# A cached attention block at decode: whole units per load, all queries and the MLP first, column tiles for V

## The chip, the cores and the metric

The kernel runs on one core of a Trainium2 chip. The metric is the device time of one execution in microseconds (us), and the figure given is the median of several runs. The profile is that of one execution, recorded by the chip's profiler; its times count from the start of the span.

## The reference

Two tokens (batch 2, one query position each) go through attention over a cache of 8192 keys in 32 heads and through a small MLP whose output gates the attention's output. Cut to what matters:

```python
# x [2,1,512]; k_cache, v_cache [2,32,8192,128]; wq [512,4096]; wo [4096,512]
# w1 [512,1376]; w2 [1376,512]; all float32
xn = layernorm(x)
q = (xn @ wq).reshape(2, 1, 32, 128).transpose(0, 2, 1, 3)
p = softmax(einsum("bhqd,bhkd->bhqk", q, k_cache) * 128 ** -0.5)
s = einsum("bhqk,bhkd->bhqd", p, v_cache).transpose(0, 2, 1, 3).reshape(2, 1, 4096) @ wo
g = silu(gelu(layernorm(xn) @ w1 + b1) @ w2 + b2)
out = x + s * g
```

K and V are 268 MB each and are read once; every byte meets one multiplication and one addition. The weights add some 22 MB.

## The kernel before

A **unit** is one (head, batch) pair: 64 units, unit i being head i // 2 and batch i % 2. K and V of a unit are 4 MB each. They come in two chunks of 2 MB (`CK` = 32 keys per partition, so 16 KB in a row for each of 128 partitions) into pools of four buffers each (`kpool`, `vpool`). All loads are issued by SyncE's queue (SP) in the order of the program; a load whose buffer isn't free yet stops all that stand behind it. K's chunks run three chunks ahead of V's (`LEAD`).

For a unit, VectorE (DVE) multiplies each chunk of K by the head's query, broadcast over the keys (L142), and sums over the 128 elements (L143). The greatest score goes from DVE (L147) through a transpose on TensorE (PE, L149) back to DVE (L154), is spread over the partitions by a product (L156) and copied by ScalarE (ACT, L158), which then takes the exponentials and their sum (L161). The denominator is a product with ones (L182) and a reciprocal (L184).

The products with V (`weighted`, L169) have four columns of exponentials as the stationary operand and four keys of V, 512 columns, as the moving one: 16 products for a unit, which float32 turns into 32 passes, all into the same 4 x 512 block of PSUM. Row r of it holds wanted sums only in its r-th block of 128 columns, which `project` picks: a copy on ACT (L193), four products with columns of the identity (L200), a scaling by the denominator (L203), and, after the second batch of a head, the product with the head's rows of `wo` (L206).

The products of a unit trail its scores: in turn i stand the second chunk of unit i-2, the projection of i-2, the maximum of i-1, and the first chunk of i-1.

The weights share `wpool`, three buffers of 1 MB: `wq` by groups of four heads (1 MB, rows of 2 KB), each loaded four units ahead of the queries that need it (`queries`, L125: sixteen passes of 512 columns for a group, since the token is spread over all 128 partitions so that the query comes out broadcast); `wo` by the same groups; and the MLP in seven parts in units 3 to 9 (`mlp_load`, `mlp_hidden`, `mlp_out`), w1 in rows of 1376 bytes (L218), w2 in rows of 2 KB (L224). The last unit's V comes in nine pieces, three of which DVE multiplies and sums itself (L175, L177).

On each engine the instructions stand in the order that a scheduler in the framework chose from this program.

Of the kernel before, what the change touches and what calls it, by code (L numbers as in the profile page):

```python
# [8 lines left out]
F32 = mybir.dt.float32  # L9
# [4 lines left out]
CK = 32          # keys per partition in one chunk of the cache  # L14
# [6 lines left out]
def decode_kernel(ctx: ExitStack, tc: tile.TileContext, x, kc, vc, wq, wo, w1, b1, w2, b2, out):  # L21
    nc = tc.nc
    P = 128
# [3 lines left out]
    ND = D // P                    # chunks of the model dimension  # L27
    KP = S // P                    # keys per partition
    NCK = KP // CK                 # chunks per (batch, head)
    HG = 512 // DH                 # heads per weight group  # L30
    NU = B * H
    SCALE = float(DH) ** -0.5
    JW = 512 // DH                 # keys per partition in one product with V

    consts = ctx.enter_context(tc.tile_pool(name="consts", bufs=1))
# [4 lines left out]
    ps_o = ctx.enter_context(tc.tile_pool(name="ps_o", bufs=2, space=bass.MemoryType.PSUM))  # L40
    ps_w = ctx.enter_context(tc.tile_pool(name="ps_w", bufs=2, space=bass.MemoryType.PSUM))
    ps_s = ctx.enter_context(tc.tile_pool(name="ps_s", bufs=3, space=bass.MemoryType.PSUM))
    ps_a = ctx.enter_context(tc.tile_pool(name="ps_a", bufs=1, space=bass.MemoryType.PSUM))

# [1 line left out]
    def load_wq(g):  # L46
        t = wpool.tile([P, ND, 512], F32, tag="w", name=f"wq{g}")
        nc.sync.dma_start(t, wq[:, g * 512:(g + 1) * 512].rearrange("(c p) n -> p c n", p=P))
        return t

    def load_wo(g):
        t = wpool.tile([P, HG, D], F32, tag="w", name=f"wo{g}")
        nc.sync.dma_start(t, wo[g * HG * DH:(g + 1) * HG * DH, :].rearrange("(h p) n -> p h n", p=P))
        return t

    def cache_chunk(t, i, c):
        h, b = divmod(i, B)
        return t[b, h, c * P * CK:(c + 1) * P * CK, :].rearrange("(p j) d -> p j d", p=P)

    def load_chunk(pool, src, name, i, c):  # L60
        t = pool.tile([P, CK, DH], F32, tag=name, name=f"{name}{i}_{c}")
        nc.sync.dma_start(t, cache_chunk(src, i, c))
        return t

    K, V, WO = {}, {}, {}
    K[0, 0] = load_chunk(kpool, kc, "k", 0, 0)
    x_sb = consts.tile([B, D], F32, name="x_sb")
    nc.sync.dma_start(x_sb, x.rearrange("b s d -> (b s) d"))
    wq_t = {0: load_wq(0)}
    for c in range(1, NCK):  # L70
        K[0, c] = load_chunk(kpool, kc, "k", 0, c)

# [4 lines left out]
    nc.vector.memset(ones, 1.0)  # L77
    srow = consts.tile([1, P], F32, name="srow")
# [17 lines left out]
    def transposed(src, n, name):  # L96
        # [B, n*128 or less] -> [128, n, B]
        p = ps_w.tile([P, 512], F32, tag="w", name=f"pt_{name}")
        t = consts.tile([P, n, B], F32, name=f"{name}T")
        width = src.shape[1]  # L100
        for c in range(n):
            m = min(P, width - c * P)
            nc.tensor.transpose(p[:m, c * B:(c + 1) * B], src[:, c * P:c * P + m], ident[:B, :B])
        full = width // P
        nc.scalar.copy(t[:, :full, :], p[:, :full * B].rearrange("p (c b) -> p c b", b=B))
        if full < n:
            m = width - full * P
            nc.scalar.copy(t[:m, full, :], p[:m, full * B:(full + 1) * B])
        return t

    xn = layernorm(x_sb, "xn")
    xnT = transposed(xn, ND, "xn")
    xnB = consts.tile([P, ND, B, P], F32, name="xnB")
    for c in range(ND):
        for b in range(B):
            nc.vector.tensor_scalar_mul(xnB[:, c, b, :], ones, xnT[:, c, b:b + 1])

# [1 line left out]
    def queries(g):  # L119
        q = small.tile([P, B, HG, DH], F32, tag="q", name=f"q{g}", bufs=2)  # L120
        w = wq_t.pop(g)
        for b in range(B):
            p = ps_w.tile([P, 512], F32, tag="w", name=f"pq{g}_{b}")
            for c in range(ND):
                nc.tensor.matmul(p, xnB[:, c, b, :], w[:, c, :], start=(c == 0), stop=(c == ND - 1))  # L125
            nc.scalar.copy(q[:, b].rearrange("p h d -> p (h d)"), p)  # L126
        return q

    Q = {0: queries(0)}

# [1 line left out]
    SC, PR, RS, MX, PO, OT = {}, {}, {}, {}, {}, {}  # L132
    PD = {}                         # partial outputs summed on VectorE
    acc = ps_a.tile([B, D], F32, name="acc")

    def scores(i, c):
        h, b = divmod(i, B)
        k = K.pop((i, c))
        if c == 0:
            SC[i] = small.tile([P, KP], F32, tag="sc", name=f"sc{i}")  # L140
# [22 lines left out]
    def weighted(i, v, k0, n, first, last, jw=JW):  # L163
        # products of n keys per partition with V as the moving operand: row r of
        # the output holds the keys k with k % jw == r in its r-th block
        if first:
            PO[i] = ps_o.tile([jw, jw * DH], F32, tag="o", name=f"po{i}")
# [19 lines left out]
    def project(i, direct=()):  # L187
# [8 lines left out]
        for v, k0, n in direct:  # L196
            terms += [(v[:, j, :], PR[i][:, k0 + j:k0 + j + 1]) for j in range(n)]
# [202 lines left out]
```

## Time and profile before

| | us |
|---|---|
| runs shown (three) | 1356.81, 1358.66, 1624.9 |
| their median | 1358.66 |
| span of the profiled execution | 1355.7 |
| DVE busy in it | 1179.7 |
| PE busy in it | 1194.9 |
| ACT busy in it | 111.3 |

The time that was taken of the profiled execution itself isn't shown apart from its span; the median of the runs stands 3.0 us above the span, the lowest run 1.1 us. The run of 1624.9 us is far from the other two, and the profile is not of it.

How to read the profile: a group of instructions is named by line, engine, operation and tiles (`po<-v,pr` writes `po` from `v` and `pr`), then count, busy time, the mean duration of one in ns, the engine's idle time just before them, and what ended it. "SPq" is the queue of loads on SyncE. A product's duration is modelled and overlaps with the next; the pace of a run of products is read from the chain of waits, which gives the time of sixteen together. "PEclk" is the clock granted to TensorE as a share of full speed. The rate in GB/s is that of all sixteen transfer engines.

### The profile page before, as it was taken

To read this page: it belongs to the slowest core of one execution; us is meant where nothing else is said; L and a number is where in the kernel's file an instruction comes from. 1 tells how busy PE (TensorE), PEld (TensorE's weight loads), DVE (VectorE), ACT (ScalarE), POOL (GpSimd) and SP (SyncE) were. 2 spreads that over 40 slices of the span, in tenths; PEclk is the share of its full clock that TensorE was granted. 3 is DMA by queue.
4 is the path that set the end of the run, shared out by engine and by line. 5 is a ranking of instruction groups with operands and counts; after the bars stand their busy time and mean duration, and the time that the engine had idled before them with its cause. 6 is when DMAs were issued, how large, how long until landed. Compare 5 with 4: busy or idle time off the path is not lost.

```text
span 1355.7 us, 7973 instructions
## 1 busy us (share of the span) xinstructions
PE 1194.9 (88%) x3191; PEld 315.5 (23%) x3191; DVE 1179.7 (87%) x491; ACT 111.3 (8%) x363; POOL 0.7 (0%) x6
## 2 busy tenths in 40 slices
PE   3598999899988989899989999899898999889897
PEld 1122222222222222122212222122222222212223
DVE  5968857989998898888989889887988879989998
ACT  0001101010000000001000000001000000000000
POOL 0000000000000000000000000000000000000000
PEclk8788899899999999889999989889988989999998
DMA  9998999999999999999999999999999999999994
GB/s 381 423 383 320 391 393 380 425 430 427 424 430 425 427 428 425 427 424 430 428 425 426 424 430 426 424 429 425 428 427 424 425 429 426 425 429 427 428 428 194
DMA packets 49922, 559.83 MB, mean 413 GB/s; under 512 B 4599, under 2 KB 6647, under 8 KB 17373
## 3 DMA queue, kind: packets, MB, share of 16 engines
q1 hardware_dynamic: 49884, 559.32, 97.9%
q8 instruction: 25, 0.41, 0.1%
q14 instruction: 13, 0.10, 0.0%
HBM read 559.30 MB, written 0.00 MB: 413 GB/s over the span
## 4 chain that ended last, share of the span: by engine, by line
PE 45%; DMA 38%; DVE 13%; ACT 3%; issue 1%; SPq 0%
PE po L169 35%; DMA v<-in_A_v_cache_dram 28%; DMA k<-in_A_k_cache_dram 9%; DVE k L142 6%; DVE sc L143 6%; PE pq L125 4%; PE pt L200 2%; PE acc L206 1%; ACT o L193 1%; PE pl L182 1%; PE pgate L264 1%; DMA x_sb<-in_A_x_dram 1%; ACT oT L203 0%; ACT pr L161 0%; PE pm L149 0%
## 5 line engine op out<-in xcount | busy, mean ns | idle before, releaser
L169 PE MATMUL po<-v,pr 128*4 128x512 f32 (+1 forms) x2076 | 955.4, 616 | 41.9 <-DMA v<-in_A_v_cache_dram 41.9
L142 DVE TENSOR_TENSOR k<-k,q 128x4096 f32<-128x4096 f32 x128 | 565.1, 4415 | 39.7 <-DMA k<-in_A_k_cache_dram 35.4
L143 DVE TENSOR_REDUCE sc<-k 128x32 f32<-128x4096 f32 x128 | 564.2, 4409 | 1.7
L169 PEld LDWEIGHTS po<-v,pr 128*4 128x4 f32 (+1 forms) x2076 | 176.0, 90 | 720.6 <-issue 667.8
L193 ACT COPY o<-po 4x512 f32<-4x512 f32 x64 | 36.4, 570 | 922.9 <-PE po L169 922.9
L200 PE MATMUL pt<-ident,o 4*128 4x1 f32 (+1 forms) x506 | 67.6, 250 | 45.8 <-ACT o L193 45.6
L200 PEld LDWEIGHTS pt<-ident,o 4*128 4x128 f32 (+1 forms) x506 | 62.1, 189 | 102.5 <-ACT o L193 102.0
L154 DVE TENSOR_REDUCE nm<-pm 1x1 f32<-1x128 f32 x64 | 17.6, 274 | 59.6 <-PE pm L149 59.5
L125 PE MATMUL pq<-wq,xnB 128*128 128x512 f32 x128 | 59.6, 617 | 1.3 <-ACT q L126 0.7
L184 DVE RECIPROCAL rl<-pl 128x1 f32<-128x1 f32 x64 | 10.3, 162 | 50.0 <-PE pl L182 50.0
L182 PE MATMUL pl<-rs,ones 128*128 128x1 f32 x128 | 28.0, 288 | 23.6 <-ACT pr L161 23.6
L206 PE MATMUL acc<-wo,oT 128*2 128x512 f32 x64 | 39.8, 709 | 4.0 <-ACT oT L203 0.4
L182 PEld LDWEIGHTS pl<-rs,ones 128*128 128x128 f32 x128 | 22.5, 220 | 60.9 <-ACT pr L161 50.8
L149 PE MATMUL pm<-ident,mx 128*1 128x128 f32 x64 | 17.4, 272 | 21.5 <-DVE mx L147 21.4
L125 PEld LDWEIGHTS pq<-wq,xnB 128*128 128x128 f32 x128 | 24.4, 197 | 30.7 <-issue 27.5
L156 PE MATMUL pb<-nm,srow 1*128 1x1 f32 x128 | 23.5, 250 | 6.2 <-DVE nm L154 6.2
L203 ACT ACTIVATE oT<-pt,rl 128x1 f32<-128x1 f32 x64 | 16.7, 261 | 83.5 <-PE pt L200 83.5
L149 PEld LDWEIGHTS pm<-ident,mx 128*1 128x1 f32 x64 | 5.1, 79 | 76.0 <-issue 48.2
L161 ACT ACTIVATE pr<-sc,bias 128x64 f32<-128x64 f32 x64 | 22.2, 348 | 2.2 <-ACT bias L158 0.2
L156 PEld LDWEIGHTS pb<-nm,srow 1*128 1x128 f32 x128 | 19.8, 192 | 7.4 <-DVE nm L154 6.5
L126 ACT COPY q<-pq 128x512 f32<-128x512 f32 x16 | 9.4, 586 | 113.0 <-PE pq L125 113.0
L147 DVE TENSOR_REDUCE mx<-sc 128x1 f32<-128x64 f32 x64 | 14.0, 219 | 1.1
(63 smaller groups left out, 106.2 us busy)
## 6 DMA issues: line engine op xcount, KB each, us to landing
k<-in_A_k_cache_dram SPq DMA_DIRECT2D x128, 2048.0 KB, 29.2
v<-in_A_v_cache_dram SPq DMA_DIRECT2D x126, 2048.0 KB, 30.3
wq<-in_A_wq_dram SPq DMA_DIRECT2D x8, 1024.0 KB, 29.4
wo<-in_A_wo_dram SPq DMA_DIRECT2D x8, 1024.0 KB, 32.4
v<-in_A_v_cache_dram SPq DMA_DIRECT2D x7, 512.0 KB, 14.8
w<-in_B_w_dram SPq DMA_DIRECT2D x4, 688.0 KB, 5.3
w<-in_B_w_dram SPq DMA_DIRECT2D x2, 1024.0 KB, 5.2
w<-in_B_w_dram SPq DMA_DIRECT2D x1, 512.0 KB, 4.0
```

What stands on the lines that cost most here:

```text
L125: nc.tensor.matmul(p, xnB[:, c, b, :], w[:, c, :], start=(c == 0), stop=(c == ND - 1))
L142: nc.vector.tensor_tensor(out=k, in0=k, in1=qb, op=ALU.mult)
L143: nc.vector.tensor_reduce(out=SC[i][:, c * CK:(c + 1) * CK], in_=k, axis=AX.X, op=ALU.add)
L149: nc.tensor.transpose(p[:1, :], mx, ident)
L154: nc.vector.tensor_reduce(out=nm, in_=MX.pop(i)[:1, :], axis=AX.X, op=ALU.max, negate=True)
L156: nc.tensor.matmul(p[:, :1], srow, nm, start=True, stop=True)
L161: nc.scalar.activation(PR[i], SC.pop(i), AF.Exp, bias=bias, scale=SCALE, accum_out=RS[i])
L169: nc.tensor.matmul(PO[i], PR[i][:, k0 + j:k0 + j + jw], v[:, j:j + jw, :].rearrange("p j d -> p (j d)"), start=(first and j == 0), stop=(l ...
L182: nc.tensor.matmul(pl[:, :1], ones, RS.pop(i), start=True, stop=True)
L193: nc.scalar.copy(o4, po)
L200: nc.tensor.matmul(pt[:, :1], lhsT, rhs, start=(t == 0), stop=(t == len(terms) - 1))
L206: nc.tensor.matmul(acc, OT.pop(h), WO[h // HG][:, h % HG, :], start=(h == 0), stop=(h == H - 1))
```

## The change

**Loads.** A unit's K and its V are one load each: 4 MB, 32 KB in a row for a partition. `kpool` has three such buffers, `vpool` two, `wpool` two of 1 MB for `wo`. In turn i stand the loads of K(i+3) and V(i+1), so K is two units ahead of V.

**Queries and MLP.** `wq` is loaded at the start, in two halves of 4 MB into V's buffers, with four of its rows to a partition; all queries are computed there (`project_q`) in column tiles, four groups of heads side by side on PSUM's partitions 0, 32, 64 and 96, and kept (`q_nat`). For each group `queries` broadcasts them by products with a column of the identity (four passes). w1 is loaded into one of K's buffers and w2 into one of V's. The hidden layer has w1 as the stationary operand: each product takes every tenth column of it, 40 bytes apart, against two columns of the token, so that the hidden values come out on the partitions and need no transposes. The output layer runs in four column tiles of 128 columns.

**Products with V.** The 16 products of a unit go in turn to four column tiles: product t writes the four PSUM partitions from 32 * (t % 4), and there are four such rows of partial sums instead of one. `mask`, four columns with ones at the right rows, sums the tiles in the projection. The product with `wo` and the final gate are in column tiles too, so output and gate lie as [4 x 32, 128].

**The end.** V of the last unit comes in five pieces; 15 products and four keys taken directly (L305); nothing of it on DVE. The last head's rows of `wo` are loaded after V's last piece. The output leaves in four stores from two queues.

**Order.** With `manual_schedule` every engine's instructions stand as the program has them: scores' multiplication of i, the maximum and exponentials of i-1, the sum of i, and then products and projection of i-2.

```diff
-CK = 32          # keys per partition in one chunk of the cache
...
-    kpool = ctx.enter_context(tc.tile_pool(name="kpool", bufs=4))
-    vpool = ctx.enter_context(tc.tile_pool(name="vpool", bufs=4))
-    wpool = ctx.enter_context(tc.tile_pool(name="wpool", bufs=3))
+    kpool = ctx.enter_context(tc.tile_pool(name="kpool", bufs=3))
+    vpool = ctx.enter_context(tc.tile_pool(name="vpool", bufs=2))
+    wpool = ctx.enter_context(tc.tile_pool(name="wpool", bufs=2))
...
+    ctx.enter_context(tc.manual_schedule())
...
+    def load_k(i):
+        K[i] = kpool.tile([P, KP, DH], F32, tag="k", name=f"k{i}")
+        nc.sync.dma_start(K[i], unit(kc, i))
...
+    PIECES = [(0, 16), (16, 16), (32, 16), (48, 12), (60, 4)]
...
+    wq_v = wq.rearrange("(p c) n -> p c n", p=P)
+    for a in range(0, ND, 2):
+        t = vpool.tile([P, 2, H * DH], F32, tag="v", name=f"wq{a}")
+        nc.sync.dma_start(t, wq_v[:, a:a + 2, :])
+        WQ.append(t)
+    load_k(0)
+    w1_sb = kpool.tile([P, ND, F], F32, tag="k", name="w1_sb")
+    nc.sync.dma_start(w1_sb, w1.rearrange("(p c) f -> p c f", p=P))
+    load_k(1)
+    w2_sb = vpool.tile([P, NF + 1, D], F32, tag="v", name="w2_sb")
...
+    load_k(2)
+    load_wo(0)
+    load_v(0)
...
+    def project_q(n):
+        p = ps_w.tile([P, 512], F32, tag="w", name=f"pq{n}")
+        for c in range(ND):
+            for j in range(QT):
+                g = n * QT + j
+                nc.tensor.matmul(p[32 * j:32 * j + B, :], xnT[:, c, :],
+                                 WQ[c // 2][:, c % 2, g * 512:(g + 1) * 512],
+                                 start=(c == 0), stop=(c == ND - 1))
...
+    def mlp_hidden():
+        p = ps_s.tile([P, P], F32, tag="s", name="ph")
+        nc.vector.memset(p[:, :(NF + 1) * B], 0.0)
+        for f in range(NF + 1):
+            for c in range(ND):
+                w = w1_sb[:, c, f:NF * P:NF] if f < NF else w1_sb[:, c, NF * P:]
+                nc.tensor.matmul(p[:w.shape[1], f * B:(f + 1) * B], w, yT[:, c, :],
+                                 start=(c == 0), stop=(c == ND - 1))
...
+    def mlp_out():
+        p = ps_s.tile([P, P], F32, tag="s", name="pgate")
+        nc.tensor.matmul(p, zeros, zeros, start=True, stop=False)
+        for f in range(NF + 1):
+            m = P if f < NF else FT
+            for j in range(QT):
+                nc.tensor.matmul(p[32 * j:32 * j + B, :], hT[:m, f, :], w2_sb[:m, f, j * P:(j + 1) * P],
+                                 start=False, stop=False)
...
+    def weighted(i, t0, t1, nt=NT):
+        po, v = PO[i % 2], V[i]
+        for t in range(t0, t1):
+            j = t % QT
+            nc.tensor.matmul(po[32 * j:32 * j + JW, :], PR[i][:, t * JW:(t + 1) * JW],
+                             v[:, t * JW:(t + 1) * JW, :].rearrange("p j d -> p (j d)"),
+                             start=(t < QT), stop=(t + QT >= nt))
...
+    for i in range(NU + 1):
+        if i + 3 < NU:
+            load_k(i + 3)
+        if i + 1 < NU:
+            if (i + 1) % UG == 0:
+                tail = load_wo((i + 1) // UG)
+            load_v(i + 1)
...
+        if i < NU:
+            scores_mul(i)
+        if i >= 1:
+            max_pe(i - 1)
+            max_dve(i - 1)
+            exps(i - 1)
+        if i < NU:
+            scores_sum(i)
+        if i >= 1:
+            denominator(i - 1)
+        if i == 0:
+            mlp_hidden()
+        if i == 1:
+            mlp_gelu()
+            mlp_out()
...
+        if i >= 2:
+            weighted(i - 2, 0, NT)
+            project(i - 2)
+    i = NU - 1
+    weighted(i, 0, NT - 1, NT - 1)
+    project(i, direct=(KP - JW, KP))
```

More of the change, by code (lines that the diff above doesn't have):

```diff
@@ L81, in decode_kernel @@
     nc.vector.memset(eps_t, EPS)
+    mask = consts.tile([P, JW], F32, name="mask")
+    PO = [ps_c.tile([P, JW * DH], F32, name=f"po{n}") for n in range(2)]
+    for t in PO:
+        nc.vector.memset(t, 0.0)
+    acc = ps_c.tile([P, P], F32, name="acc")
     def layernorm(src, name):
@@ L94, in layernorm, with transposed @@
         return dst
[L96 to L108, printed above, removed]
+    def transposed(src, name):
+        p = ps_s.tile([P, P], F32, tag="s", name=f"pt_{name}")
+        t = consts.tile([P, ND, B], F32, name=f"{name}T")
+        for c in range(ND):
+            nc.tensor.transpose(p[:, c * B:(c + 1) * B], src[:, c::ND], ident[:B, :B])
+        nc.scalar.copy(t, p[:, :ND * B].rearrange("p (c b) -> p c b", b=B))
@@ L129, in decode_kernel @@
[L129 to L136, printed above, removed]
+    nc.vector.tensor_reduce(out=mask, in_=ident.rearrange("p (j r) -> p r j", r=32)[:, :JW, :],
+                            axis=AX.X, op=ALU.add)
+    y = layernorm(xn, "y")
+    xnT = transposed(xn, "xn")
+    yT = transposed(y, "y")
+    q_nat = consts.tile([P, NG // QT, 512], F32, name="q_nat")
+    nc.gpsimd.memset(q_nat, 0.0)
+    def project_q(n):
[6 more added lines that the diff above has]
+                                 start=(c == 0), stop=(c == ND - 1))
+        for j in range(QT):
+            nc.scalar.copy(q_nat[32 * j:32 * j + B, n, :], p[32 * j:32 * j + B, :])
@@ new lines, in decode_kernel, with queries @@
+    Q = {}
+    def queries(g):
+        n, j = divmod(g, QT)
+        q = small.tile([P, B, HG, DH], F32, tag="q", name=f"q{g}", bufs=2)
+        for b in range(B):
+            p = ps_w.tile([P, 512], F32, tag="w", name=f"pb{g}_{b}")
+            r = 32 * j + b
+            nc.tensor.matmul(p, ident[:, r:r + 1].to_broadcast([P, P]), q_nat[:, n, :], start=True, stop=True)
+            nc.scalar.copy(q[:, b].rearrange("p h d -> p (h d)"), p)
+        Q[g] = q
+    project_q(0)
+    queries(0)
+    project_q(1)
@@ L157, in max_b, with exps @@
+    def exps(i):
+        p = ps_s.tile([P, P], F32, tag="s", name=f"pn{i}")
+        nc.tensor.matmul(p[:, :1], srow, MX.pop(i), start=True, stop=True)
         bias = small.tile([P, 1], F32, tag="bias", name=f"bias{i}")
@@ new lines, in project @@
+            for j in range(QT):
+                nc.tensor.matmul(acc[32 * j:32 * j + B, :], oT, w[:, h % HG, j * P:(j + 1) * P],
+                                 start=False, stop=(h == H - 1))
+    for i in range(NU + 1):
[5 more added lines that the diff above has]
+            load_v(i + 1)
+        if i == NU - 2:
+            nc.sync.dma_start(tail[0][:, HG - 1, :], tail[1][:, HG - 1, :])
+        if i < NU:
[13 more added lines that the diff above has]
+            mlp_out()
+        if i == 2:
+            mlp_silu()
+        if i % UG == UG - 2 and i // UG + 1 < NG:
+            queries(i // UG + 1)
@@ L369, in decode_kernel @@
-    r = small.tile([B, D], F32, tag="res", name="res", bufs=1)
+    i = NU - 1
+    weighted(i, 0, NT - 1, NT - 1)
+    project(i, direct=(KP - JW, KP))
+    r = small.tile([P, P], F32, tag="res", name="res", bufs=1)
     nc.vector.tensor_mul(r, acc, gate)
-    nc.vector.tensor_add(r, r, x_sb)
-    nc.sync.dma_start(out.rearrange("b s d -> (b s) d"), r)
+    nc.vector.tensor_add(r, r, x4)
+    for j in range(QT):
+        eng = nc.sync if j % 2 == 0 else nc.scalar
+        eng.dma_start(out[:, 0, j * P:(j + 1) * P], r[32 * j:32 * j + B, :])
```

313 lines of the change are left out of this document (94 added, 219 removed).

## The prediction

> **What bounds the kernel now.** The page came first: the span, the slices of transfer rate and the queue's bytes.
>
> ```profile
> span 1355.7 us, 7973 instructions
> ...
> GB/s 381 423 383 320 391 393 380 425 430 427 424 430 425 427 428 425 427 424 430 428 425 426 424 430 426 424 429 425 428 427 424 425 429 426 425 429 427 428 428 194
> ...
> q1 hardware_dynamic: 49884, 559.32, 97.9%
> ```
>
> The rate is flat from the eighth slice on, lower in the first seven and in the last. A table by stretches (columns: stretch, busy time of PE, weight loads, DVE, ACT, POOL, then granted clock, DMA share, GB/s) prices this:
>
> ```profile
> 3.00:240.00 237.00, 188.52 (x494) 51.43 (x495) 181.93 (x94) 25.54 (x73) 0.00 (x0) 0.88 0.94 386
> 240.00:1320.00 1080.00, 977.51 (x2556) 250.60 (x2554) 968.78 (x378) 81.13 (x277) 0.00 (x0) 0.94 1.01 427
> 1320.00:1338.00 18.00, 17.10 (x65) 5.72 (x64) 16.36 (x8) 2.57 (x9) 0.00 (x0) 1.00 0.95 391
> 1338.00:1356.00 18.00, 11.76 (x82) 7.71 (x79) 12.35 (x10) 0.78 (x3) 0.00 (x0) 0.77 0.05 17
> ```
>
> For 1080 us the transfer engines are never idle: the kernel is bound by its 559.32 MB, which at 427 GB/s take 1309.9 us. The other 46 us are start, stalls and tail. Between 3 and 240 us 386 GB/s instead of 427 lose 237 x 41/427 = 22.8 us; behind the last bytes, at about 1338, stand 17.7 us; the rest is the start and 1.5 us ahead of 1338. Where the 22.8 us go, the transfer slices of the first 240 us (6 us each) and the load queue's own waits say:
>
> ```profile
> GB/s 235 421 406 429 431 350 431 431 406 443 431 426 342 248 429 429 418 352 437 429 300 33 423 429 429 221 407 434 434 307 401 426 436 377 207 394 431 414 431 434
> ```
>
> ```profile
> SPq L62 <- DVE sc L143: 340.7, 57, 23.0
> ...
> SPq L218 <- PE ph L243: 58.7, 3, 22.1
> SPq L224 <- PE pgate L264: 30.1, 2, 18.6
> SPq L224 <- PE ph L243: 19.3, 1, 19.3
> ```
>
> The dips are MLP weight loads (L218, L224) standing at the head of the in-order SP queue until TensorE frees a weight buffer: 108 us of waiting, of which the queue's depth hides all but some 20. The first slice, 235, puts the start of the stream at 6 x (1 - 235/427) = 2.7 us.
>
> **The change, part by part.** Everything is priced by when the next transfer can start.
>
> *Stream.* The bytes stay; rows go from 16 to 32 KB, wq, w1 and w2 from rows of 1.4 or 2 KB to 16 KB and more; only wo keeps 2 KB. No row shows 32 KB. The lower bound is the steady slices in which 2 KB rows still lie, 424; the upper one the 6 us slices at 434. 424 gives 1319.1 us, 434 gives 1288.8. I take 429, nearest to the undisturbed steady slices (427 to 430): 1303.8 us.
>
> *DVE and PE in a unit.* The page's groups, one line of the V tile's own rows, and the chain of waits:
>
> ```profile
> L142 DVE TENSOR_TENSOR k<-k,q 128x4096 f32<-128x4096 f32 x128 | 565.1, 4415 | 39.7 <-DMA k<-in_A_k_cache_dram 35.4
> L143 DVE TENSOR_REDUCE sc<-k 128x32 f32<-128x4096 f32 x128 | 564.2, 4409 | 1.7
> ...
> L193 ACT COPY o<-po 4x512 f32<-4x512 f32 x64 | 36.4, 570 | 922.9 <-PE po L169 922.9
> ...
> L154 DVE TENSOR_REDUCE nm<-pm 1x1 f32<-1x128 f32 x64 | 17.6, 274 | 59.6 <-PE pm L149 59.5
> ...
> L184 DVE RECIPROCAL rl<-pl 128x1 f32<-128x1 f32 x64 | 10.3, 162 | 50.0 <-PE pl L182 50.0
> ...
> L156 PE MATMUL pb<-nm,srow 1*128 1x1 f32 x128 | 23.5, 250 | 6.2 <-DVE nm L154 6.2
> ...
> L161 ACT ACTIVATE pr<-sc,bias 128x64 f32<-128x64 f32 x64 | 22.2, 348 | 2.2 <-ACT bias L158 0.2
> ...
> L147 DVE TENSOR_REDUCE mx<-sc 128x1 f32<-128x64 f32 x64 | 14.0, 219 | 1.1
> ```
>
> ```profile
> L175 DVE TENSOR_TENSOR v<-v,pr x4: 1207/1210/3360, 1330.5 to 1345.9; 128x1024 f32<-128x1024 f32 x3, 128x3072 f32<-128x3072 f32 x1
> ```
>
> ```profile
> 11.76 6.10 PE pq L125 x8
> 17.88 0.59 ACT q L126
> ...
> 86.47 1.06 PE pt L200 x8
> ...
> 384.91 7.04 PE po L169 x16
> ...
> 606.82 6.87 PE pq L125 x16
> ```
>
> From 3072 to 4096 elements a multiply grows by 1.055 us, so 8192 take about 8.7, the reduction the same: 17.4 + 0.27 + 0.16 + 0.22 = 18.1 us of DVE per unit against two loads of 4.19 MB / 429 = 19.6. DVE stays behind the loads with 1.5 us to spare, and may start late: 64 x 18.1 = 1158 us, so unit 63 waits for its K as before. An unpaired product pass costs 7.04/16 = 0.44 us; a unit has 32. One at a time they are 14.1 us, and with about 3 us of small work (the projection's 1.06, the weights' rows and the three single products) they still fit under 19.6. The queries of a group shrink from sixteen passes (6.87 us) to four, a gain on an engine that isn't the bound. How far four column tiles overlap no row shows: bounds 14.1 us and a quarter of it, 3.5. I take about 5, nearer to the low end since the four write different partitions and share no weights.
>
> The Trainium skill, page "TensorE: Matmul & The Clock Gate", section "Measured speedup vs the span model", has three column tiles at 2.38 times one; by that the products would take 14.1/2.38 = 5.9 us, and the sum would be 1 us longer. Against the change speaks its page "TensorEngine Tiling (Array Packing)", section "Key Properties": a change of tiling mode drains TensorE, here twice a unit; no row shows one.
>
> A steady unit on PE, before (L182 the denominator, L169 products of a half unit, L149 the transpose of the maxima, L200 the projection):
>
> ```order
> L182 MATMUL pl_2681<-rs_2679,ones 128x1
> L169 MATMUL po_2687<-v_0_2650,pr_2678 4x512 x8
> L149 MATMUL pm_2698<-ident,mx_2696 1x128
> L169 MATMUL po_2687<-v_1_2702,pr_2678 4x512 x8
> L200 MATMUL pt_2721<-ident,o_41_2719 128x1 x4
> ```
>
> And after (L260 transpose, L270 maximum, L277 denominator, L292 products, L305 projection):
>
> ```order
> L260 MATMUL pm_470<-ident,mx_433 1x128
> L270 MATMUL pn_474<-nm_472,srow 128x1
> L277 MATMUL pl_481<-rs_479,ones 128x1
> L292 MATMUL po_128<-v_277,pr_426 4x512 x16
> L305 MATMUL pt_507<-mask,o_2_505 128x1 x4
> ```
>
> The transpose for unit i-1 now stands behind all products of unit i-3. These begin about 10.5 us after k(i-1) lands (8.7 multiply, 0.3 maximum, 1.5 for the exponentials: two passes of L156, a copy, L161, hand-offs) and end 14.1 + 3 later at worst, 27.6, while DVE reaches its maximum at 19.6 + 8.7 = 28.3. So that wait costs nothing even without overlap; were it late, the K buffers would cover it, since K(i+3) needs the sum of K(i) only some 30 us after it. V(i+1) needs the buffer of V(i-1), freed at the latest 44 us after K(i) landed (28.3 + 1.5 + 14.1) and needed 59 after it (three units on): hidden too. Steady state has no gap.
>
> *Head.* SP's first loads before (wq, wo a group's weights; k, v half units):
>
> ```order
> L62 DMA k_0_82<-in_A_k_cache_dram 128x4096
> L68 DMA x_sb<-in_A_x_dram 2x512
> L48 DMA wq_86<-in_A_wq_dram 128x4x512
> L62 DMA k_1_88<-in_A_k_cache_dram 128x4096
> L53 DMA wo_150<-in_A_wo_dram 128x4x512
> L62 DMA k_0_152<-in_A_k_cache_dram 128x4096
> L62 DMA k_1_154<-in_A_k_cache_dram 128x4096
> L62 DMA v_0_156<-in_A_v_cache_dram 128x4096
> ```
>
> And after, from the second half of wq to the second load of V (k, v whole units; the two w_sb of L90 and L93 are w1 and w2):
>
> ```order
> L86 DMA wq_85<-in_A_wq_dram 128x8192
> L58 DMA k_87<-in_A_k_cache_dram 128x8192
> L90 DMA w_sb<-in_B_w_dram 128x5504
> L58 DMA k_91<-in_A_k_cache_dram 128x8192
> L93 DMA w_sb<-in_B_w_dram 128x5120
> L94 DMA w_sb<-in_B_w_dram 96x512
> L58 DMA k_96<-in_A_k_cache_dram 128x8192
> L64 DMA wo_98<-in_A_wo_dram 128x4x512
> L74 DMA v_100<-in_A_v_cache_dram 128x8192
> L58 DMA k_220<-in_A_k_cache_dram 128x8192
> L74 DMA v_222<-in_A_v_cache_dram 128x8192
> ```
>
> All of wq and the MLP's weights moved into the first dozen loads, sharing K's and V's buffers. Laid end to end from 2.7 us the stream ends: wq 22.2, k0 32.0, w1 38.5, k1 48.3, w2 54.8, k2 64.6, wo 67, v0 76.8, k3 86.6. What frees buffers, with rows for PE's pace:
>
> ```profile
> 1346.22 1.05 PE L200 MATMUL pt<-pr,v 128*128 128x1 f32 x8
> ```
>
> The query projection starts when wq's second half lands at 24: sixteen cold passes at 0.76 are 12.2 us singly, 3 in four tiles; then five copies of 0.59 and four passes, so q is there at 33 to 42. k0 is usable at 34; DVE ends unit 0 at 51.6, in time for k2 (54.8 less some 2 us of issue and landing). Then PE runs the hidden layer, 88 passes at 0.13 us (1.05/8) = 11.5 us with contiguous weights; w1's columns are now 40 bytes apart, which no row shows, so 11.5 to 35 (0.4 each). A gain is excluded, since the loads read no fewer weights. I take 0.2: ends at 69.5, in time for k3 (74.8). But unit 0's transpose stands behind it, so DVE waits: maximum 70, sum 78.7, GELU 81, then 96 output passes of 128 columns at 0.12 (a quarter of 0.44, and the 0.13 of small passes): 92.5. Only then is w2's buffer free for v1: first bytes at 94.5 against 86.6, a gap of 8 us, 2 at 0.13 per pass. Queued behind v1 on SP is everything else, K's loads too. With 1 us of lesser gaps, 9. The 22.8 us of before go. The seven small loads moved to ACT's queue (x, b1, b2) are needed at 79 us or later; the slowest first load of before, x_sb, took 7.29 us, so they are covered tenfold.
>
> *Tail.* Rows of before's end, of its first small load and of a load into an empty queue:
>
> ```profile
> 1349.73 0.27 ACT oT L203
> ...
> 1350.05 1.88 PE acc L206 x2
> ...
> 1351.95 0.69 DVE res L370
> ```
>
> ```profile
> 1.19 7.29 DMA x_sb<-in_A_x_dram
> ```
>
> ```profile
> w<-in_B_w_dram SPq DMA_DIRECT2D x2, 1024.0 KB, 5.2
> ```
>
> ```profile
> 1353.37 0.27 SPq L372 DMA_DIRECT2D out_dram<-res  x1
> ```
>
> The second last gives issue and landing: 5.2 less 1.05 MB / 427 = 2.7 us; the last the store, 1355.7 - 1353.4 = 2.3.
>
> From k63's landing T three V loads are left. v63 waits for the products of unit 61: maximum at T+9, exponentials T+10.5, products T+15.5, with issue and landing T+18 against the end of v62 at T+19.6: a gap of 1 at most. Products 62 end at T+26; those of 63 follow their pieces. Behind the last bytes: landing 2, three products 0.5, copy 0.6, 16 small passes 2, scale 0.3, wo 1, two DVE operations of 128 columns 0.5, store 2.3: 9.2, with the gap 10, instead of 17.7 + 1.5. Were PE still cold, these passes and the products of 61 to 63 take up to twice as long: 20. The DVE sums over V's last pieces, which carried the old tail, are gone; late next is PE's projection.
>
> Sum: 2.7 + 1303.8 + 9 + 10 = 1325.5 us of span. The runs' median, 1358.66, stands 3.0 above the profiled span (the lowest, 1356.81, 1.1 above): **1328 us**.
>
> **Rivals.** *Rows make no difference.* Loads of twice the size stay where steady slices with 2 KB rows lie, 424 to 427, and gains come from head and tail alone: 1309.9 to 1319.1, + 21.7 + 3 = 1335 to 1344. For it: 2 KB rows lower a slice by 3 to 6 GB/s at most, so row length may be no lever. 0.12. The Trainium skill, "DMA: Bandwidth & Descriptors", section "Measured", has 425 GB/s for its largest transfer, 16 MB; by that the time would be 1316.0 + 24.7 = 1341. The trace has 427 with 2 MB, above it already.
>
> *Column tiles don't overlap*, so the change doesn't do what it says. Steady state holds, but the ends lengthen: head 17 (projection of the queries and the output passes serial); in the tail products 61 end at T+24.6, those of 62 at T+43, those of 63 at T+57, and 7 us later, T+64, all ends, where the bytes alone would end at T+30: 34. 2.7 + 1303.8 + 17 + 34 + 3 = 1360, no change. 0.14.
>
> *Strided weights.* At 0.4 us a pass the hidden layer ends at 87, k3 starts 12 us late, v1 14 more: head 26, 1345. 0.13.
>
> *TensorE becomes the bound, slower.* In the stretch
>
> ```profile
> 20.00:40.00 20.00, 1.61 (x7) 0.53 (x6) 20.00 (x5) 0.65 (x2) 0.00 (x0) 0.59 0.99 405
> ```
>
> the clock is 0.59 where PE idles, and eight cold passes took 6.10 us, 0.76 each. If PE idles between units and column-tiled passes run one at a time at that pace, a unit is 32 x 0.76 + 3 = 27.3 us, some 1780 us in all. It decides slower from (20.7 - 3)/32 = 0.55 a pass. Against: work that fills PE was granted 0.94. With mixtures of the two rivals above, 0.09.
>
> **Numbers.** The forecast, 0.52, spans 1308 (434 GB/s, head 4) to 1332. A measurement here tells about 2% from no change: faster means under 1331.5, slower over 1385.8. Faster 0.52, same 0.39 (three rivals), slower 0.09. The range 1308 to 1358 leaves out the slower case, half of the no-overlap case and 0.03 below.
>
> **What would show it.** No slice under 420 GB/s between 110 and 1280 us; steady slices at 429 or more (427 or less: first rival); sixteen products in about 5 us, and within 14 in any case; one gap near 87 us at v1's load, released by the output passes of the MLP; about 9 us behind the last bytes. Wrong would be a steady slice below 420, PE busy all along, or a load queue waiting for PE in steady state.

## The result: 1319.88 us, 0.972 of the time before

| | before | after |
|---|---|---|
| median of the runs, us | 1358.68 | 1319.88 (1317.93 to 1320.07) |
| after / before | | 0.9719, 95% interval 0.9705 to 0.9734 |
| profiled execution: its time, span, us | span 1355.7 | 1319.86, 1318.1 |
| PE busy, mean granted clock | 1194.9 us, 0.927 | 586.5 us, 0.643 |

The kernel became 2.8% faster; 1328 was predicted. One run of the kernel before, 1624.9 us, lies far from its others and is not in the ratio. The page of the new kernel, in the lines that answer to those of before:

```profile
span 1318.1 us, 8108 instructions
...
PE 586.5 (44%) x3434; PEld 226.1 (17%) x3434; DVE 1143.7 (87%) x348; ACT 110.7 (8%) x353; POOL 1.6 (0%) x7
...
GB/s 392 421 424 431 432 432 427 431 431 433 430 428 429 432 432 433 428 430 431 432 430 427 432 432 429 433 425 436 432 429 428 431 430 432 428 432 431 431 431 252
...
q1 hardware_dynamic: 23948, 559.30, 99.1%
```

The dips of the first seven slices are gone, and the flat part is higher. The table by stretches of the new kernel (columns as in the prediction: stretch, busy time of PE, weight loads, DVE, ACT, POOL, then granted clock, DMA share, GB/s):

```profile
3.00:240.00 237.00, 112.47 (x674) 54.22 (x678) 193.91 (x69) 23.79 (x67) 0.00 (x0) 0.68 1.00 426
240.00:1280.00 1040.00, 451.04 (x2613) 163.10 (x2605) 930.88 (x264) 83.13 (x274) 0.00 (x0) 0.63 1.00 431
```

The span is 37.6 us shorter. Three places account for that:

- **Head.** In 237 us 40 GB/s more were moved, 9.5 MB, which at the old 427 GB/s are 22 us.
- **Steady part.** The 458 MB that are left at 240 us come at 431 instead of 427 GB/s: 1072.6 - 1062.6 = 10 us.
- **Tail.** What remains is some 5 us. (A rate is rounded to 1 GB/s, which is up to 1.2 us in the steady part and so in this remainder.)

So it is still transfers that bound the kernel, now from the third microsecond on; TensorE's busy time was halved, and that was not what was being waited for. The waits of the load queue in the new kernel (us in total, times, longest):

```profile
SPq L74 <- DMA v<-in_A_v_cache_dram: 651.5, 59, 14.0
SPq L74 <- PE po L292: 458.5, 61, 15.9
SPq L58 <- DVE rl L282: 39.5, 41, 1.7
SPq L93 <- PE pq L168: 21.3, 1, 21.3
...
SPq L74 <- PE pgate L231: 15.4, 1, 15.4
```

V's load stands still in nearly every unit, first 11 us on average for an earlier V to land, then 7.5 us for TensorE's products, and the transfers don't notice: while it stands, the loads ahead of it are still running (DMA share 1.00 above). A wait in the load queue is a cost only where the transfers run out, and of that the slices are the witness, not the wait.

### The profile page after: what moved, and what is told of

It is laid out like the page before. It is cut to its first block, busy times and chain, and to the rows that moved or that the text cites. A ratio compares the mean times of both kernels' runs of the same rounds, so it can differ in the third digit from the quotient of the medians.

```text
span 1318.1 us, 8108 instructions
## 1 busy us (share of the span) xinstructions
PE 586.5 (44%) x3434; PEld 226.1 (17%) x3434; DVE 1143.7 (87%) x348; ACT 110.7 (8%) x353; POOL 1.6 (0%) x7
## 4 chain that ended last, share of the span: by engine, by line
DMA 64%; DVE 27%; PE 8%; ACT 1%; issue 0%; SPq 0%; DVEq 0%
DMA k<-in_A_k_cache_dram 55%; DVE k L250 15%; DVE sc L254 11%; DMA v<-in_A_v_cache_dram 8%; PE po L292 5%; PE ph L204 1%; DMA wq<-in_A_wq_dram 1%; PE pb L183 1%; PE pn L270 0%; PE pl L277 0%; PE pt L305 0%; ACT pr L275 0%; DVE nm L265 0%; SPq L74 0%; ACT o L300 0%
## 5 line engine op out<-in xcount | busy, mean ns | idle before, releaser
L250 DVE TENSOR_TENSOR k<-k,q 128x8192 f32<-128x8192 f32 x64 | 556.2, 8691 | 135.6 <-DMA k<-in_A_k_cache_dram 109.9
L254 DVE TENSOR_REDUCE sc<-k 128x64 f32<-128x8192 f32 x64 | 554.9, 8671 | 0.0
L292 PE MATMUL po<-v,pr 128*4 128x512 f32 x2046 | 353.6, 853 | 10.3 <-DMA v<-in_A_v_cache_dram 10.3
L270 PE MATMUL pn<-nm,srow 1*128 1x1 f32 x128 | 36.8, 354 | 571.7 <-DVE nm L265 571.7
L270 PEld LDWEIGHTS pn<-nm,srow 1*128 1x128 f32 x128 | 31.8, 307 | 585.3 <-DVE nm L265 423.7
L292 PEld LDWEIGHTS po<-v,pr 128*4 128x4 f32 x2046 | 58.0, 107 | 255.2 <-issue 243.5
L305 PE MATMUL pt<-mask,o 128*128 128x1 f32 x512 | 67.4, 253 | 45.7 <-ACT o L300 45.7
L305 PEld LDWEIGHTS pt<-mask,o 128*128 128x128 f32 x512 | 61.9, 191 | 108.1 <-ACT o L300 108.1
L300 ACT COPY o<-po 128x512 f32<-128x512 f32 x64 | 37.5, 586 | 395.4 <-PE po L292 395.4
L183 PE MATMUL pb<-q_nat,ident 128*128 128x512 f32 x32 | 29.9, 1089 | 2.6 <-ACT q_nat L172 2.6
L204 PE MATMUL ph<-yT,w_sb 128*128 128x2 f32 (+1 forms) x88 | 19.5, 359 | 13.7 <-DVE ph L200 13.7
L256 DVE TENSOR_REDUCE mx<-sc 128x1 f32<-128x64 f32 x64 | 14.1, 220 | 2.2
```

The lines of the kernel that those rows point to most:

```text
L183: nc.tensor.matmul(p, ident[:, r:r + 1].to_broadcast([P, P]), q_nat[:, n, :], start=True, stop=True)
L204: nc.tensor.matmul(p[:w.shape[1], f * B:(f + 1) * B], w, yT[:, c, :], start=(c == 0), stop=(c == ND - 1))
L250: nc.vector.tensor_tensor(out=k, in0=k, in1=qb, op=ALU.mult)
L254: nc.vector.tensor_reduce(out=SC[i], in_=K.pop(i), axis=AX.X, op=ALU.add)
L270: nc.tensor.matmul(p[:, :1], srow, MX.pop(i), start=True, stop=True)
L292: nc.tensor.matmul(po[32 * j:32 * j + JW, :], PR[i][:, t * JW:(t + 1) * JW], v[:, t * JW:(t + 1) * JW, :].rearrange("p j d -> p (j d)"), s ...
```

## The experiments

In the runs of the experiments the kernel before had medians of 1357.6 to 1357.9 us; ratios are to it, with their 95% intervals.

### Column tiles taken away

```diff
-            j = t % QT
+            j = 0
...
-                             start=(t < QT), stop=(t + QT >= nt))
+                             start=(t == 0), stop=(t == nt - 1))
```

> The new kernel with all sixteen products of a unit in the first column tile, one after another. Theory (transfers bound the steady state; column tiles count in the tail alone): the slices between 110 and 1240 us stay at 430 GB/s or more; 32 passes take about 14 us instead of 5.4 to 6.4, at a higher clock; the last V load starts about 8 us later, products of the last two units follow one another, and the time is 1335 to 1346 us, all of the addition behind 1280 us. Rival 1 (the tiles take TensorE off the path in steady state): over 1355 us, with steady slices under 425. Rival 2 (the tiles change nothing): 1320 within 3.

Measured: 1354.69 us, 0.9981 (0.9967 to 0.9995). The products in one column tile cost 35 us, nearly the whole gain. But where? The steady part of the change, then of this kernel:

```profile
300.00:1200.00 900.00, 393.30 (x2270) 142.15 (x2262) 805.52 (x228) 73.01 (x239) 0.00 (x0) 0.63 1.00 430
...
300.00:1200.00 900.00, 806.06 (x2251) 213.32 (x2249) 805.03 (x226) 72.95 (x239) 0.00 (x0) 0.91 1.00 430
```

PE is busy for 806 of 900 us instead of 393, and the rate is still 430. The end of its chain of waits (start, duration, what) shows where the time went:

```profile
1297.60 13.84 PE po L292 x32
...
1315.96 15.54 PE po L292 x32
...
1333.21 12.98 PE po L292 x30
```

The multiply of the last K starts at 1285.96 instead of 1278.13 us, so some 8 us are lost before it, most of them in the first 240 us (411 instead of 423 GB/s); some 27 are lost behind it, where three units' products stand one behind another with no transfer left to hide them. Column tiles are worth nothing in the steady part and most in the tail. The place was as expected for the 27 us only, and the size was not, since the serial products of the last three units alone are 42 us.

### Column tiles given to the kernel before

Its products go to four column tiles in all units but the last two; everything else stays (core of the edit):

```diff
-            PO[i] = ps_o.tile([jw, jw * DH], F32, tag="o", name=f"po{i}")
+            PO[i] = PB[i % 2][:jw, :jw * DH]
...
+                r = 32 * (t % 4)
+                nc.tensor.matmul(PO[i][r:r + jw, :], PR[i][:, k0 + j:k0 + j + jw],
+                                 v[:, j:j + jw, :].rearrange("p j d -> p (j d)"),
+                                 start=(t < 4), stop=(t + 4 >= KP // jw))
```

> The kernel before with the products with V in four column tiles (all units but the last two), nothing else. Theory (TensorE is not on the path in steady state): products take about 6 instead of 14 us of a unit, PE's busy time falls by a third or more, and the time stays at 1358 within 5. Rival (the tiles are what made the new kernel faster): 1320 to 1335.

Measured: 1362.82 us, 1.0039 (1.0025 to 1.0054), 5 us slower. From its table by stretches:

```profile
0.00:240.00 240.00, 127.04 (x504) 38.85 (x504) 180.01 (x99) 27.16 (x74) 0.70 (x6) 0.70 0.91 375
240.00:1320.00 1080.00, 593.41 (x2542) 185.22 (x2542) 974.29 (x378) 83.77 (x277) 0.00 (x0) 0.61 1.01 427
```

PE's busy time there falls from 977.5 to 593.4 us, and the rate is the 427 of before. Faster products alone buy nothing where transfers bound. Some 4 of the 5 us lie in the first 240, where 375 instead of 382 GB/s are moved and w2's loads wait 68 us for the MLP's buffers instead of 49; why they wait longer isn't shown.

### Row length: 16 and 8 KB

The same 4 MB loads, of K and of V, cut along the keys into two transfers of 16 KB rows, or four of 8 KB (K's edit for 16 KB):

```diff
-        nc.sync.dma_start(K[i], unit(kc, i))
+        for k0 in range(0, KP, 32):
+            nc.sync.dma_start(K[i][:, k0:k0 + 32, :], unit(kc, i)[:, k0:k0 + 32, :])
```

> The new kernel with each 4 MB load as two transfers of 16 KB rows into the same buffer, in the same places of the queue. Theory (the longer rows raised the steady rate): steady slices fall to about 427 GB/s and the time rises by 8 to 12 us, to 1328 to 1332. Rival (the steady rate rose because the small rows of the weights are gone from it): slices stay at 431 and the time within 3 us of 1320.

> The same with four transfers of 8 KB rows each. Theory (a fixed time of about 10 ns for each row of a transfer engine, worked out from 427 at 16 KB and 431 at 32 KB): about 421 GB/s in steady state and 1346 to 1354 us. Rival (rows from 8 KB on cost nothing): 1320 within 3, or as the run with 16 KB rows.

Measured: 1327.65 us, 0.9785 (0.9766 to 0.9803), and 1347.19 us, 0.9928 (0.9907 to 0.9948). The steady part with 16 KB rows:

```profile
300.00:1200.00 900.00, 388.15 (x2247) 141.23 (x2251) 802.06 (x226) 72.09 (x237) 0.00 (x0) 0.63 1.01 427
```

and with 8 KB rows:

```profile
300.00:1200.00 900.00, 380.52 (x2208) 139.17 (x2212) 790.75 (x223) 71.24 (x235) 0.00 (x0) 0.64 1.01 421
```

The rate falls with the row's length, 430, 427, 421. But both kernels also have more transfers; the next one has not.

### Row length with one transfer

One load of 4 MB still, but each partition takes two rows of 16 KB from two places (core of the edit):

```diff
-        return t[b, h].rearrange("(p j) d -> p j d", p=P)
+        return t[b, h].rearrange("(c p j) d -> p c j d", c=2, p=P)
```

> The new kernel with each unit of K and V as one load of 4 MB whose rows are 16 KB: two for a partition, from the two halves of the unit, so the keys lie in another order, for K and V alike. Theory (a row costs a transfer engine a fixed 8 to 10 ns, however many rows a load has): about 428 GB/s in steady state and 1326 to 1330 us, as with two loads of 16 KB rows each. Rival (it is the number of loads that cost the 8 us): 1320 within 2.

Measured: 1328.05 us (1326.95 to 1329.48), 0.9787 (0.9769 to 0.9805), at 427 GB/s in its steady part: the same as with two transfers. So the length of a row counts; the number of transfers shows no effect. The price: K's and V's 127 whole loads have 127 x 128 rows more, 1016 for each of 16 transfer engines; 7.8 and 8.2 us by that are 8 ns a row, and the 27.3 us of the 8 KB kernel by 3048 rows are 9. The kernel before has 16 KB rows and 427 GB/s, as these two: its lower steady rate is explained. Whether its 2 KB rows of `wq` and `wo` cost something on top wasn't tried.

### The MLP's loads in the kernel before, spread out

One part of the MLP in every second unit instead of every unit, in the kernel before; nothing else:

```diff
-        part = i - MLP_AT
+        part = (i - MLP_AT) // 2 if i >= MLP_AT and (i - MLP_AT) % 2 == 0 else -1
```

> The kernel before with the seven MLP parts in every second unit (3 to 15) instead of in each of units 3 to 9; the same loads, the same work. Theory (the 22.8 us lost before 240 us are the load queue standing at MLP weight loads that wait for a buffer): the loads find their buffers free, the queue's waits at L218 and L224 fall from 108 us to under 30, and the time falls by 12 to 20 us, to 1339 to 1347. Rival (the slow start has another cause: short rows of the weights, the cold start of the engines): 1358 within 4.

Measured: 1341.47 us, 0.9883 (0.9859 to 0.9907), 16.4 us faster, within what was expected. The first 240 us of the kernel before, then this kernel's first 240 us and its steady part:

```profile
0.00:240.00 240.00, 188.52 (x494) 51.43 (x495) 182.23 (x97) 26.82 (x74) 0.70 (x6) 0.89 0.93 382
...
0.00:240.00 240.00, 187.31 (x489) 49.69 (x490) 194.58 (x102) 25.17 (x71) 0.70 (x6) 0.88 1.00 418
240.00:1320.00 1080.00, 993.76 (x2604) 255.53 (x2603) 968.72 (x381) 84.96 (x288) 0.00 (x0) 0.94 1.01 425
```

From 382 to 418 GB/s are 20 us of transfers. The waits at the MLP's loads fall from 108 to 25 us: those of w2's loads (L224) to 5.5, those of w1's (L218) to 19.5, of which one of 15.8 is for a buffer that a group of queries held. The steady part gives some 5 us back, at 425 instead of 427 GB/s, and no run shows why. So the head's loss was what the prediction took it for, loads that stand at the head of an in-order queue until a weight buffer is free. Most of the largest part of the gain could have been had by one line.

### V's load ahead of K's

From unit 8 on, V(i+1) stands ahead of K(i+3) in the load queue instead of behind it:

```diff
-        if i + 3 < NU:
+        if i + 3 < NU and i < UG:
             load_k(i + 3)
...
             load_v(i + 1)
+        if i + 3 < NU and i >= UG:
+            load_k(i + 3)
```

> The new kernel with V(i+1) ahead of K(i+3) in the queue from the ninth turn on, so that K is one unit ahead of V instead of two. Theory (the lead is covered in steady state and counts at the end, where the last K stands two loads from the end of the stream instead of three while DVE and PE need 40 us behind it): steady slices unchanged, 7 to 10 us longer, 1327 to 1330. Rival (the lead keeps the steady state free of gaps): steady slices under 425 and over 1345 us. Rival 2: no change, 1320 within 3.

Measured: 1363.32 us, 1.0041 (1.0024 to 1.0057). The theory expected the lead to count at the end only, for 7 to 10 us, and it fell: it had one part of the loss right and not the larger one. The multiply of the last K starts at 1323.72 instead of 1278.13 us, 45.6 later. Of these 9.4 are K's later place behind one more load (unit 12 starts at 277.87 instead of 268.44), and the other 36 build up in the steady part, where the 51 units from there on take 1045.9 us instead of 1009.7. What follows the last K became 2 us shorter. The timeline of this kernel in the middle, DVE's multiplies (start, duration, what, idle time before and its releaser):

```profile
606.10 8.69 DVE L250 TENSOR_TENSOR k<-k,q 128x8192 f32<-128x8192 f32 x1 [1.62 <-DMA k<-in_A_k_cache_dram]
626.66 8.69 DVE L250 TENSOR_TENSOR k<-k,q 128x8192 f32<-128x8192 f32 x1 [2.76 <-DMA k<-in_A_k_cache_dram]
647.90 8.69 DVE L250 TENSOR_TENSOR k<-k,q 128x8192 f32<-128x8192 f32 x1 [3.43 <-DMA k<-in_A_k_cache_dram]
...
667.36 8.69 DVE L250 TENSOR_TENSOR k<-k,q 128x8192 f32<-128x8192 f32 x1 [1.65 <-DMA k<-in_A_k_cache_dram]
```

and its load queue:

```profile
623.00 0.33 SPq L74 DMA_DIRECT2D v<-in_A_v_cache_dram  x1
623.42 0.38 SPq L58 DMA_DIRECT2D k<-in_A_k_cache_dram  x1
643.55 0.33 SPq L74 DMA_DIRECT2D v<-in_A_v_cache_dram  x1
643.98 0.38 SPq L58 DMA_DIRECT2D k<-in_A_k_cache_dram  x1
```

A K lands at 606.1. Its multiply must pass before DVE takes the maximum of the unit before, and behind that unit's denominator stand, on PE, the products that free a V buffer: V is issued at 623.0, 17 us after the landing, and K right behind it. That K is the one that DVE waits for until 647.9, 24.5 us after its issue: the two loads, 19.5 us, and 5 for issue, landing and what was still running of the load before. A loop from landing to landing takes some 41 us (626.66 to 667.36), and it spans two units, 20.4 each. Two loads at 430 GB/s take 19.5, so the loop sets the pace, and not the transfers. In the change's own order K is one unit further ahead of V: the same loop of 41 us spans three units, for which the transfers need 58.5, and has 17 us to spare. The two units of lead are what lets the load queue wait 458 us for TensorE at no cost.

### The fixed order taken away

The scheduler orders the new program:

```diff
-    ctx.enter_context(tc.manual_schedule())
```

> The new kernel without the fixed order: the framework's scheduler puts the instructions. Theory (order matters at head and tail only, transfers bound the rest): 1314 to 1330, steady slices at 431. Rival (the fixed order is what keeps the steady state free of gaps): over 1335, with steady slices under 425.

Measured: 1378.74 us, 1.0162 (1.0137 to 1.0186), 59 us slower than with the order. That it would make no difference was expected, and the rival was right. One unit of this kernel in its timeline (lines are one lower: L249 the multiply, L253 the sum, L255 and L264 the maximum, L281 the reciprocal):

```profile
598.79 8.68 DVE L249 TENSOR_TENSOR k<-k,q 128x8192 f32<-128x8192 f32 x1
...
607.50 8.69 DVE L253 TENSOR_REDUCE sc<-k 128x64 f32<-128x8192 f32 x1
...
616.91 0.28 DVE L264 TENSOR_REDUCE nm<-pm 1x1 f32<-1x128 f32 x1 [0.46 <-PE pm L259]
...
619.26 0.17 DVE L281 RECIPROCAL rl<-pl 128x1 f32<-128x1 f32 x1 [2.08 <-PE pl L276]
619.35 8.67 DVE L249 TENSOR_TENSOR k<-k,q 128x8192 f32<-128x8192 f32 x1
```

The whole chain of the maximum stands between the sum of one unit and the multiply of the next. DVE waits there for PE and ACT, and a unit takes 619.35 - 598.79 = 20.56 us, more than the 19.5 of its two loads. After the first unit DVE waits for no K any more: DVE is the bound, 64 x 20.56 = 1316 us. In the fixed order that chain lies beside the next multiply and sum, and a unit of DVE's work takes 17.8.

### Strided weights

The hidden layer takes 128 neighbouring columns of w1 instead of every tenth (timed once):

```diff
-                w = w1_sb[:, c, f:NF * P:NF] if f < NF else w1_sb[:, c, NF * P:]
+                w = w1_sb[:, c, f * P:(f + 1) * P] if f < NF else w1_sb[:, c, NF * P:]
```

> The new kernel whose hidden layer takes 128 neighbouring columns of w1 for a product instead of every tenth; the hidden values then stand in another order than b1 and w2 expect, so the MLP's output is not the reference's. Theory A (the 0.22 us of a hidden pass is the weight load at half clock): L204 stays at 19 to 20 us for 88 passes, a weight load at 310 to 320 ns. Theory B (it is the 40-byte step): 11 to 13 us, 190 ns. Time within 3 us of 1320 by both.

Measured: 1318.03 us. The groups of the two kernels, first of the change, then of this one (the 88 products of the layer; busy, mean ns | idle before):

```profile
L204 PE MATMUL ph<-yT,w_sb 128*128 128x2 f32 (+1 forms) x88 | 19.5, 359 | 13.7 <-DVE ph L200 13.7
```

```profile
L204 PE MATMUL ph<-yT,w_sb 128*128 128x2 f32 (+1 forms) x88 | 18.5, 347 | 14.7 <-DVE ph L200 14.7
```

The stride of 40 bytes costs at most 1 us in 19 at this clock. What makes a pass 0.22 us, in both kernels, is in all likelihood the granted clock, here in the change's table by stretches:

```profile
60.00:80.00 20.00, 13.25 (x59) 12.55 (x59) 8.76 (x3) 1.88 (x4) 0.00 (x0) 0.50 1.00 421
```

Eight passes of the projection (L305) at 1306.77 us, with weights of the same size, take 1.05 us, 0.13 each, where 1.00 is granted.

### The tail: a warm TensorE, and a buffer for the last V

In the change, TensorE has little to do while the last K is multiplied, and the last V waits for a V buffer. Two edits and both together: eight products of zeros in the last unit, whose result nobody reads, and the last V in one of K's buffers, which are free by then.

```diff
+    def warm(n):
+        p = ps_w.tile([P, 512], F32, tag="w", name="warm")
+        for _ in range(n):
+            nc.tensor.matmul(p[:JW, :], zeros[:, :JW], q_nat[:, 0, :], start=True, stop=True)
...
+            if i == NU - 1:
+                warm(8)
```

```diff
-        V[i] = vpool.tile([P, KP, DH], F32, tag="v", name=f"v{i}")
+        if i < NU - 1:
+            V[i] = vpool.tile([P, KP, DH], F32, tag="v", name=f"v{i}")
+        else:
+            V[i] = kpool.tile([P, KP, DH], F32, tag="k", name=f"v{i}")
```

> The new kernel with eight more products of 512 columns, of zeros, in TensorE's turn 63, into a spare PSUM tile that nothing reads, where it waits about 10 us for the maximum of unit 62. Theory (the end is a chain of TensorE work behind the last K, run at half clock): the clock rises, the products of units 61 and 62 take about 4 instead of 6 us each, the last V load starts 2 to 3 us earlier, and the time falls by 2 to 4 us, to 1316 to 1318. Rival (the chain's waits for VectorE and the last bytes take up what the clock gives): within 1 us of 1319.9. If the added products outlast the wait, up to 2 us longer.

> The new kernel with the V of the last unit in one of K's buffers, which nothing else needs any more, so that its load no longer waits for the products of unit 61. Theory (the 3 us in which no bytes move before the last V load are not what sets the end; TensorE's chain is): the gap at 1296 us goes, the bytes end about 3 us earlier, and the time stays within 1 us of 1319.9. Rival (the gap sets the end): 2 to 4 us less.

> Both edits together, the added products of zeros and the last V in one of K's buffers. Theory: as with the added products alone or up to 1 us less, 1315 to 1318, since the earlier load matters only once the chain is short. Rival (each is worth its own 3 us): 1313 to 1315.

Measured: 1318.44 us, 0.9715 (0.9697 to 0.9733); 1318.39 us, 0.9721 (0.9703 to 0.9739); both 1317.38 us, 0.9712 (0.9694 to 0.9730). All three intervals overlap that of the change, so no gain of theirs can be told from none. Each edit alone came out between its theory and its rival, both together where the theory had them, and the 1313 to 1315 us that the rival gave both were not reached. The traces do show what the edits did. With the added products, the clock in the last multiply is 0.89 instead of 0.50:

```profile
1280.00:1290.00 10.00, 6.49 (x22) 1.75 (x24) 10.00 (x3) 0.60 (x3) 0.00 (x0) 0.89 0.98 423
```

and the products of the third last unit take 4.93 us instead of 6.34. The added products don't raise the clock, they hold it: in both kernels the products of the unit before had brought it to 0.99 by 1274 to 1277 us; from 1280 to 1287 it is 1.00 here and 0.50 in the change. With the other buffer the last V is issued at 1274.83 instead of 1295.37, and the dip of the rate goes from 302 to 400 GB/s:

```profile
1290.00:1300.00 10.00, 7.84 (x58) 2.60 (x53) 6.38 (x5) 1.45 (x5) 0.00 (x0) 0.84 0.95 400
```

But the clock in this stretch is 0.84 too, against 0.67 in the change, and nothing in the edit explains that; a part of what it gains may be chance. The transfers end earlier and the products are what ends last, which is why filling the gap returns little. How far the tail could be shortened stays open.

## Why the prediction was right, and where its sizes were off

It gave 1328 for 1319.88, by way of a sum whose terms can each be compared. All terms are of the profiled execution.

| term | predicted, us | measured, us |
|---|---|---|
| start of the stream | 2.7 | 2.3 |
| stream | 1303.8 (429 GB/s) | 1301 (430 GB/s) |
| gaps in the head | 9 | 2 |
| tail: gap and what follows the last bytes | 1 + 9.2 | 3 + 9.6 |
| own time less span | 3.0 | 1.8 |

**Stream.** Right. The middle was put between 424 and 434 by nearness to rows of before, without a row for 32 KB, so that it came within 1 or 2 GB/s is in part luck. The rival that rows make no difference is refuted by the three kernels with shorter rows, though its time (1335 to 1344) was too long even so: with 16 KB rows the new kernel takes 1327.65 us. That is the forecast of 1328, so the time alone couldn't have told the two apart; the rate did. The 425 GB/s that the Trainium skill states, in "DMA: Bandwidth & Descriptors", section "Measured", for its largest transfer is passed by the steady part of the kernel before, 427, and of the change, 430 to 431.

**Head.** The right gap, and mis-sized: it is the term that makes up most of the error. The prediction let the MLP's output layer run 96 passes at 0.12 us, to 92.5, and V's load wait for that 8 us. The timeline of the change, the hidden layer, the output layer and that load:

```profile
51.70 19.50 PE L204 MATMUL ph<-yT,w_sb 128*128 128x2 f32 x88 [13.65 <-DVE ph L200]
...
82.14 4.54 PE L228 MATMUL pgate<-w_sb,hT 128*2 128x128 f32 x88 [6.52 <-DVE hT L220]
...
86.75 0.33 SPq L74 DMA_DIRECT2D v<-in_A_v_cache_dram  x1
```

The hidden layer ended at 71.2 for 69.5 predicted (0.22 us a pass for 0.2). The output layer, whose price had been a quarter of a serial pass with no allowance for its four column tiles, took 4.54 / 88 = 0.052 a pass. So the load went out at 86.75, a moment after the 86.6 at which the prediction had the stream run dry. The slices of the first 240 us (6 us each) show what is left of the gap, 363 in the fifteenth; over the whole stretch 426 instead of 430 GB/s are the 2 us of the table:

```profile
GB/s 263 438 437 415 415 410 442 437 427 389 396 461 437 426 363 437 431 431 426 418 437 431 426 437 438 431 431 430 426 437 437 431 431 423 431 437 431 395 440 431
```

The rival of the strided weights (1345, at 0.4 us a pass) fell with the 0.22 measured and with the kernel that reads them contiguously.

**Products.** Some 5 us a unit had been taken from bounds of 3.5 and 14.1. The group of the change, and two of its units in the timeline:

```profile
L292 PE MATMUL po<-v,pr 128*4 128x512 f32 x2046 | 353.6, 853 | 10.3 <-DMA v<-in_A_v_cache_dram 10.3
```

```profile
616.43 6.40 PE L292 MATMUL po<-v,pr 128*4 128x512 f32 x32
...
639.31 3.62 PE L292 MATMUL po<-v,pr 128*4 128x512 f32 x32
```

That is 353.6 / 64 = 5.5 on average. At best four tiles are 13.84 / 3.62 = 3.8 times as fast as the one of the first experiment, more than the 2.38 that the Trainium skill has for three tiles ("TensorE: Matmul & The Clock Gate", "Measured speedup vs the span model"). The rival that tiles don't overlap gave 1360 us; the kernel built so, for the products with V alone, took 1354.7, and the steady part held, as that rival had said.

**Steady state without a gap.** Right, and by the working given: DVE waits 1.6 us for K in most units, for 1.5 predicted.

```profile
605.61 8.69 DVE L250 TENSOR_TENSOR k<-k,q 128x8192 f32<-128x8192 f32 x1 [1.62 <-DMA k<-in_A_k_cache_dram]
```

No slice between 110 and 1280 us is under 425, where the signs had asked for 420; seven of the 34 are under the 429 that they asked of steady slices, and the mean is 430 to 431. One sign of error that the prediction named, a load queue that waits for PE in steady state, is there and cost nothing: 458.5 us of it. The sign should have been a slice of the rate that falls.

**Tail.** The end of the change's chain of waits:

```profile
1278.13 8.69 DVE k L250
...
1289.01 6.34 PE po L292 x32
...
1300.28 5.83 PE po L292 x32
...
1307.82 3.58 PE po L292 x30
...
1312.06 1.96 PE pt L305 x16
...
1315.15 0.29 DVE res L356
```

and its table by stretches there:

```profile
1280.00:1290.00 10.00, 2.12 (x12) 1.25 (x16) 10.00 (x3) 0.60 (x3) 0.00 (x0) 0.50 1.00 433
1290.00:1300.00 10.00, 7.84 (x49) 2.70 (x41) 6.19 (x4) 1.45 (x5) 0.00 (x0) 0.67 0.76 302
...
1290.00:1292.00 2.00, 2.00 (x12) 0.30 (x8) 2.00 (x1) 0.00 (x0) 0.00 (x0) 0.50 0.84 360
1292.00:1294.00 2.00, 2.00 (x12) 0.30 (x8) 2.00 (x1) 0.00 (x0) 0.00 (x0) 0.50 0.68 295
```

The step "products T+15.5" came at T+17.2 (T is 1278.1): at a clock of 0.50 these products took 6.3 us and not 5. The gap was some 3 us and not 1. The later products explain only a part of it: with the last V issued at T+17.3 and 2.7 us to its landing by the prediction's price, T+20.0 stands against T+19.6, where it had the load before end. But the rate falls from 1290 us on, T+12, with 0.84 and 0.68 of the transfer engines busy: some of them have nothing left to move several us before the others, and a single end for that load leaves this out. That TensorE might be cold there was in the prediction, as the upper end of the tail, and it was partly so. What follows the last bytes was 9.6 for 9.2.

**TensorE as the bound.** The premise of the slower rival came true, its consequence did not: PE idles for more than half of the time and is granted 0.63, but its products overlap at that clock too, 6.40 us for 32 passes instead of 24.3 (27.3 with 3 us of small work). The 0.76 us a pass behind that price were called cold, but they were taken at 11.76 us, and the table by stretches has 1.00 for 10 to 20 us: what made those passes slow isn't shown.

**What the argument lacked.** It took the fixed order and the lead as means without a price and asked only whether the change did harm with them. The tiles it did price, in the rival that they don't overlap, at 1360 - 1328 = 32 us. Each of the three, taken away alone, eats the gain of 39 us or nearly so: 59, 43 and 35 us. None of them makes the kernel fast; they keep three K buffers and two V buffers of 4 MB from making it slow.

## What to carry to other kernels

Coarser loads mean fewer buffers, and then the chain from a load's landing to the release of the buffer that the next load waits for must fit into the transfers that the order puts between them: follow it instruction by instruction, count how many units it spans, and compare with the time of their loads, since one place in the order was 43 us here. A load that may have to wait should not stand at the head of an in-order queue with nothing running behind it; look at the slices of the rate, not at the length of the wait. Work that is hidden in the middle can show at the end, so price the last units of a pipeline by themselves.

## What the runs showed that was not expected

- Between rows of 8, 16 and 32 KB, each row more costs a transfer engine 8 to 9 ns, whether the rows come in one transfer or in several.
- TensorE that is busy for 19.5 us without a pause, but only with weight loads of 128 columns and products of two, is granted 0.50 throughout (the hidden layer, 51.7 to 71.2 us); eight products of 512 columns, 7 us of work, held a clock of 1.00 that falls to 0.50 without them.
- Weights read at steps of 40 bytes load as fast as neighbouring ones at that clock, 316 ns a load against 328; at a higher clock it wasn't tried.
- Passes of 128 columns in four column tiles follow one another every 52 ns.
